# Cutting one early store into nine pieces instead of six, with other DMA engines chosen

## The chip, the core and the metric

One core of one Trainium2 chip runs the program. The metric is the device time of one execution in microseconds (us), as the median of several runs.

## What is computed

The kernel computes single-query attention and its gradients for 32 heads, 8192 keys and head size 128, all bfloat16:

```python
def _fwd_reference(q, k, v):                 # q 1x32x1x128, k and v 1x32x8192x128
    scale = q.shape[-1] ** -0.5
    scores = jnp.einsum('bhqd,bhkd->bhqk', q, k) * scale
    attn = _softmax(scores, axis=-1)
    return jnp.einsum('bhqk,bhkd->bhqd', attn, v)

def reference(q, k, v, grad_out):            # out, dq, dk, dv
    _out, _vjp = jax.vjp(_fwd_reference, q, k, v)
    return (_out, *_vjp(grad_out))
```

K and V are read once (67 MB each) and dK and dV are written once (67 MB each). With one query per head, dV is the outer product of the attention row and grad_out, and dK is the outer product of the score gradient and q.

## The kernel before, in words

The heads are handled in 16 pairs. One pair's K or V is a tile of 128 partitions, and each partition holds 128 "slots" (rows of K or V) of 128 bfloat16, so 32 KB per partition and 4096 KB per tile. The kernel has three K buffers and two V buffers. For pair j it transposes K on VectorE, computes the scores on TensorE, takes the softmax, contracts with V, and then overwrites the V tile in place with dV (`outer(j, "dv", r)`, eight steps of 16 slots each). One pair later the K tile is overwritten with dK in the same way. So a buffer is free for the next load only when its store has landed.

Nearly all DMAs are issued by SyncE (SP) in a fixed order that is written out by hand. SP works through its list in order: a DMA that has to wait for a semaphore holds back everything behind it. The part of the list around the change is: load of K of pair 2 (two halves), store of slots 64 to 127 of dV of pair 0 (L299), store of dK of pair 0 (L305), load of V of pair 2 (`load_v(2)`, L93), store of dV of pair 1 (two halves), load of K of pair 3. V of pair 2 goes into the buffer of V of pair 0, so `load_v(2)` waits until every DMA of dV of pair 0 has landed.

Slots 0 to 63 of dV of pair 0 are the exception (L296 and L297): GpSimd (POOL) issues them. They are 128 rows, one for each partition, of 16 KB each. `share_out` cuts the rows into the pieces listed in `SHARES`. An entry is (engine, first, n): the n partitions first, first + 3, first + 6 and so on go out as one DMA. The program assumes that a DMA of n rows is laid on k neighbouring DMA engines, where k is the largest divisor of n that is at most 16, beginning at a cursor that moves on by k with each GpSimd DMA. `turn_to(engine)` puts the cursor where the next piece is to begin: it issues a load of a few bytes per row into `turned` (L111) with as many rows as the cursor has to move. So each piece (L120) has one such turn ahead of it where the cursor is not yet in its place, and 128 rows can be shared unevenly among the 16 DMA engines. A SP transfer, by contrast, has 128 partitions and is shared evenly.

GpSimd DMAs take turns on eight completion semaphores. The compiled program therefore has the ninth GpSimd DMA wait until the first has landed, the tenth until the second has landed, and so on.

Of the kernel before, what the change touches and what calls it, by code (L numbers as in the profile page):

```python
# [23 lines left out]
QD = 32  # L24
LOADS = {("k", 0): 4, ("v", 0): 2, ("v", 1): 4, ("k", 2): 2}
SHARED = 64
SHARES = ((6, 12, 39), (5, 2, 42), (5, 1, 8), (15, 55, 25), (10, 25, 10), (7, 0, 4))
GP = 4


# [1 line left out]
def kernel(  # L32
# [70 lines left out]

    turned = consts.tile([17, len(SHARES), 2, 2], BF16)
    cursor = [0, 0]

    def turn_to(engine):
        n = (engine - cursor[0]) % 16
        if n:
            rows = n if n > 1 else 17  # L110
            nc.gpsimd.dma_start(turned[0:rows, cursor[1]],  # L111
                                k[0, 0].rearrange("(p n) d -> p n d", p=P)[0:rows, 0:2, 0:2])
            cursor[1] += 1
        cursor[0] = engine

    def share_out(dst, src):
        for engine, first, n in SHARES:
            turn_to(engine)
            last = first + 3 * n - 2
            nc.gpsimd.dma_start(dst[first:last:3], src[first:last:3], max_dma_last_dim=8192)  # L120
            cursor[0] = (cursor[0] + max(i for i in range(1, 17) if n % i == 0)) % 16
# [403 lines left out]
```

## Time and profile before

| | before |
|---|---|
| time, median of 3 runs | 633.09 us (632.57 to 633.21) |
| time of the profiled execution | 632.87 us |
| its span (first to last recorded work) | 631.1 us |
| VectorE busy | 516.4 us, 82% |
| TensorE matmul busy | 462.9 us, 73% |
| ScalarE busy | 205.1 us, 32% |
| GpSimd busy | 11.3 us, 2% |
| bytes moved by DMA | 268.98 MB, mean 426 GB/s over the span |
| DMA packets of SP's queue (q1) | 11232 packets, 98.5% of the time of 16 DMA engines |
| DMA packets of GpSimd's queue (q0) | 800 packets, 0.8% |

The span is 1.77 us shorter than the profiled execution's own time; what lies between is start and end of the execution, outside the recorded work. Times in the profile count from the start of the span. "Landing" is the time from the issue of a DMA until its semaphore has its full count.

### The profile page before, as it was taken

The page shows a single profiled execution, that of the slowest core. Times are in us where ns is not written, and L with a number is a line of the kernel's source. Part 1 is how long each engine was busy: PE and PEld are TensorE (multiplying, and loading weights), DVE is VectorE, ACT ScalarE, POOL GpSimd, SP SyncE. Part 2 cuts the span into 40 slices and gives each one's busy share as a digit, 9 for nine tenths or more (in the row PEclk, how much of TensorE's full clock was granted, in tenths as well). Part 3 has the DMA queues.
Part 4 walks back from the last instruction along what each step waited for, and adds up shares of the span by engine and source line. Part 5 has one row for each costly group of instructions (what it writes and reads, how often), then busy time and mean ns, then how long its engine had stood idle before and what let it go on. Part 6 is the DMA issues. An engine that isn't in the chain of part 4 may idle for free.

```text
span 631.1 us, 8018 instructions
## 1 busy us (share of the span) xinstructions
PE 462.9 (73%) x3256; PEld 245.9 (39%) x3256; DVE 516.4 (82%) x654; ACT 205.1 (32%) x460; POOL 11.3 (2%) x23
## 2 busy tenths in 40 slices
PE   4887678878787788676888757867679776697671
PEld 1443344244443425233363432624336243262441
DVE  6579997989889798796879959879697895987973
ACT  2432424043342505134052330613316142160431
POOL 2040000000000000000000000000000000000000
PEclk9789987789798977788868789777897778987785
DMA  8999999999999999999999999999999999999997
GB/s 366 433 402 436 430 428 431 429 427 440 433 427 436 436 431 433 433 432 429 429 432 429 427 433 427 433 432 418 431 430 437 436 431 425 436 427 431 428 426 336
DMA packets 12164, 268.98 MB, mean 426 GB/s; under 512 B 1856, under 2 KB 1888, under 8 KB 1888
## 3 DMA queue, kind: packets, MB, share of 16 engines
q1 hardware_dynamic: 11232, 266.34, 98.5%
q0 software_dynamic: 800, 2.12, 0.8%
q8 instruction: 25, 0.41, 0.2%
q14 instruction: 11, 0.09, 0.0%
q10 hardware_dynamic: 96, 0.02, 0.0%
HBM read 134.23 MB, written 134.23 MB: 425 GB/s over the span
## 4 chain that ended last, share of the span: by engine, by line
issue 91%; DMA 3%; PE 3%; DVE 1%; ACT 0%; POOL 0%; POOLq 0%; ACTq 0%
DMA out_dram<-Vt 2%; PE s_ps L198 1%; DMA Kt<-in_k_dram 1%; PE T_ps L215 1%; PE acc_p L265 0%; DVE XK_sb L188 0%; DVE Vt L290 0%; POOL out_dram L120 0%; DVE q_blk L174 0%; ACT p_rep L452 0%; DVE sT L205 0%; ACT win L255 0%; ACT e L440 0%; POOL turned L111 0%; POOLq L520 0%
## 5 line engine op out<-in xcount | busy, mean ns | idle before, releaser
L198 PE MATMUL s_ps<-XK_sb,q_win 128*128 128x512 bf16 x512 | 152.4, 432 | 66.6 <-DVE XK_sb L188 61.3
L290 DVE TENSOR_TENSOR Vt<-p_rep,qd 128x2048 bf16<-128x2048 bf16 x128 | 154.0, 1223 | 40.1 <-PE acc_p L265 32.2
L188 DVE STREAM_TRANSPOSE XK_sb<-Kt 128x1024 f32<-128x1024 f32 x128 | 150.2, 1218 | 37.7 <-DMA Kt<-in_k_dram 35.0
L215 PE MATMUL T_ps<-ident_f,Vt 128*128 128x128 f32 x1024 | 165.4, 314 | 6.1 <-DMA Vt<-in_v_dram 6.1
L220 ACT COPY XV_sb<-T_ps 128x512 f32<-128x512 f32 x256 | 139.6, 591 | 82.6 <-PE T_ps L215 82.4
L290 DVE TENSOR_TENSOR Kt<-ds_rep,qd 128x2048 bf16<-128x2048 bf16 x128 | 149.5, 1215 | 3.2 <-PE acc_ds L265 2.8
L215 PEld LDWEIGHTS T_ps<-ident_f,Vt 128*128 128x128 f32 x1024 | 131.2, 160 | 43.8 <-issue 18.7
L198 PEld LDWEIGHTS <-q_win 128*128 128x128 bf16 x512 | 51.6, 110 | 155.6 <-issue 123.9
L265 PE MATMUL acc_p<-Vt,win 128*32 128x512 bf16 x512 | 55.9, 439 | 2.8 <-ACT win L255 2.8
L440 ACT ACTIVATE e<-sT,nbias 128x128 f32<-128x128 f32 x16 | 8.2, 515 | 150.6 <-DVE nbias L436 150.6
L265 PEld LDWEIGHTS <-win 128*32 128x32 bf16 x1024 | 23.0, 99 | 60.6 <-issue 49.4
L265 PE MATMUL acc_ds<-Kt,win 128*32 128x512 bf16 x512 | 42.7, 429 | 4.6 <-ACT win L255 4.6
L232 PE MATMUL dp_ps<-XV_sb,do_win 128*32 128x512 bf16 x512 | 34.3, 383 | 13.5 <-ACT XV_sb L220 13.5
L255 ACT COPY win<-ds 64x128 bf16<-64x128 bf16 x32 | 9.5, 296 | 106.4 <-DVE ds L327 106.2
L232 PEld LDWEIGHTS <-do_win 128*32 128x32 bf16 x512 | 14.3, 94 | 29.2 <-issue 22.5
L441 PE MATMUL m_ps<-rs,ones_f 128*128 128x1 f32 x32 | 7.5, 305 | 24.4 <-ACT e L440 24.4
L427 PE MATMUL m_ps<-ident_f,top 128*128 128x128 f32 x16 | 4.8, 300 | 23.5 <-DVE top L425 23.5
L205 DVE STREAM_TRANSPOSE sT<-s_ps 128x512 f32<-128x512 f32 x16 | 11.5, 717 | 10.7 <-PE s_ps L198 10.7
L441 PEld LDWEIGHTS m_ps<-rs,ones_f 128*128 128x128 f32 x32 | 6.2, 242 | 27.6 <-ACT e L440 27.6
L452 ACT ACTIVATE p_rep<-e,rinv 128x512 bf16<-128x512 f32 x16 | 11.5, 722 | 13.3 <-DVE rinv L450 13.3
L427 PEld LDWEIGHTS m_ps<-ident_f,top 128*128 128x128 f32 x16 | 2.1, 133 | 31.0 <-issue 25.4
L317 PEld LDWEIGHTS m_ps<-pd,ones_f 128*128 128x128 f32 x32 | 8.2, 276 | 10.6 <-DVE prod L248 9.8
(60 smaller groups left out, 158.1 us busy)
## 6 DMA issues: line engine op xcount, KB each, us to landing
Kt<-in_k_dram SPq DMA_DIRECT2D x14, 4096.0 KB, 29.1
Vt<-in_v_dram SPq DMA_DIRECT2D x14, 4096.0 KB, 29.0
out_dram<-Kt SPq DMA_DIRECT2D x13, 4096.0 KB, 25.1
out_dram<-Vt SPq DMA_DIRECT2D x13, 4096.0 KB, 32.3
out_dram<-Vt SPq DMA_DIRECT2D x5, 2048.0 KB, 16.2
out_dram<-Kt SPq DMA_DIRECT2D x5, 2048.0 KB, 15.7
Kt<-in_k_dram SPq DMA_DIRECT2D x4, 1024.0 KB, 8.2
Vt<-in_v_dram SPq DMA_DIRECT2D x2, 2048.0 KB, 17.5
```

Of the source, the lines that this page charges most:

```text
L188: nc.vector.transpose(XK[j, u][:].rearrange("p g w i -> p (g w i)"), slots(Kt[j], u, NU).rearrange("p g d -> p (g d)").bitcast(F32))
L198: nc.tensor.matmul(st[j]["s"][:], lhsT=q_win[:, c, at:at + P], rhs=cols[:, c // 2, c % 2], start=(u == 0 and c == 0), stop=(u == NU - 1 an ...
L205: nc.vector.transpose(sT[:].rearrange("p g r -> p (g r)"), x["s"][:])
L215: nc.tensor.transpose(T_ps[:, i, :], words[:, m * P:(m + 1) * P], ident_f[:])
L220: nc.scalar.copy(XV[j][:, b * TB:(b + 1) * TB, :], st[j].pop(("T", c))[:])
L232: nc.tensor.matmul(out[b * QD:(b + 1) * QD, :], lhsT=do_win[:, b // 2, e2, at:at + QD], rhs=cols[:, z, e2, :, b * QD:(b + 1) * QD], start= ...
L255: nc.scalar.copy(win[t * M:(t + 1) * M, :, at:at + 4], src[t * M:(t + 1) * M])
L265: nc.tensor.matmul(acc[which][b * QD:(b + 1) * QD, :], lhsT=win[:, g, at:at + QD], rhs=X[:, 4 * g:4 * g + 4, :].rearrange("p n d -> p (n d)"),
L290: nc.vector.tensor_tensor(slots(G, r, NU).rearrange("p n (a b) -> p n a b", b=R), slots(rep, r, NU).unsqueeze(2).to_broadcast([P, CH, D // ...
L317: nc.tensor.matmul(x["m"][:, 1:3], lhsT=ones_f[:], rhs=x["pd"][:], start=True, stop=True, skip_group_check=True)
L441: nc.tensor.matmul(x["m"][:, 0:1], lhsT=ones_f[:], rhs=rs[:], start=True, stop=True, skip_group_check=True)
L452: nc.scalar.activation(x["p"][:], e[:].unsqueeze(2).to_broadcast([P, NT, R]), ACT.Copy, scale=rinv[:])
```

## The change

One line changes, the table of the pieces. Nothing else in the program differs: the instructions of TensorE, VectorE, ScalarE and SP are the same in the same order, and on GpSimd the twelve DMAs of `share_out` (six turns, six pieces) become eighteen (nine turns, nine pieces).

```diff
-SHARES = ((6, 12, 39), (5, 2, 42), (5, 1, 8), (15, 55, 25), (10, 25, 10), (7, 0, 4))
+SHARES = ((6, 13, 39), (6, 12, 39), (15, 29, 25), (5, 2, 7), (5, 0, 4), (7, 104, 8), (7, 1, 2), (2, 23, 2), (7, 7, 2))
```

The turns before the pieces have 6, 2, 2, 2, 6 and 3 rows before the change, and 6, 3, 12, 17, 9, 14, 8, 9 and 3 rows after it (17 rows, a prime, stand for a cursor that has to move by one). By the rule that the program assumes, the 128 rows are shared among the DMA engines like this:

| DMA engine | 0 | 1 | 2 | 3 | 4 | 5 | 6 | 7 | 8 | 9 | 10 | 11 | 12 | 13 | 14 | 15 |
|---|---|---|---|---|---|---|---|---|---|---|---|---|---|---|---|---|
| rows before | 12 | 12 | 12 | 6 | 0 | 4 | 7 | 8 | 8 | 8 | 9 | 8 | 8 | 7 | 7 | 12 |
| rows after | 11 | 11 | 12 | 6 | 0 | 2 | 8 | 11 | 11 | 8 | 8 | 8 | 7 | 7 | 7 | 11 |

## The prediction, made before the changed kernel was run

> **What bounds the kernel now.** I read the page first, its slices and queues.
>
> ```profile
> DMA  8999999999999999999999999999999999999997
> ...
> q1 hardware_dynamic: 11232, 266.34, 98.5%
> q0 software_dynamic: 800, 2.12, 0.8%
> ```
>
> The first line is the mean busy share of the 16 DMA engines in 40 slices; the two others are queue, packets, MB and share of 16 engines' time. The DMA engines are full from the second slice to the last but one, 98.5% with SP's transfers alone. So the end is set by DMA: a compute engine matters only where it leaves a DMA engine without work. Next I read GpSimd's instructions in order of time around the change (start, length, what, idle time before it), and then the landing times of the DMAs issued between 30 and 65 us (the last number).
>
> ```profile
> 32.13 0.65 POOL L120 DMA_DIRECT2D out_dram<-Vt  x1 [27.97 <-DVE Vt L290]
> 32.78 0.58 POOL L111 DMA_DIRECT2D turned<-in_k_dram  x1
> 33.35 0.62 POOL L120 DMA_DIRECT2D out_dram<-Vt  x1
> ...
> 41.53 0.56 POOL L120 DMA_DIRECT2D out_dram<-Vt  x1 [4.61 <-DMA out_dram<-Vt]
> 42.16 0.73 POOL L111 DMA_DIRECT2D turned<-in_k_dram  x1
> 45.80 0.59 POOL L120 DMA_DIRECT2D out_dram<-Vt  x1 [2.91 <-DMA out_dram<-Vt]
> ```
>
> ```profile
> out_dram<-Kt SPq DMA_DIRECT2D x1, 4096.0 KB, 21.9
> out_dram<-Vt SPq DMA_DIRECT2D x1, 2048.0 KB, 26.2
> out_dram<-Vt POOLq DMA_DIRECT2D x1, 672.0 KB, 12.2
> out_dram<-Vt POOLq DMA_DIRECT2D x1, 624.0 KB, 9.1
> out_dram<-Vt POOLq DMA_DIRECT2D x1, 400.0 KB, 21.3
> out_dram<-Vt POOLq DMA_DIRECT2D x1, 160.0 KB, 18.7
> ...
> out_dram<-Vt POOLq DMA_DIRECT2D x1, 64.0 KB, 17.3
> ```
>
> The last two pieces wait: the fifth (160 KB, 10 rows) until the first piece has landed (32.13 + 9.1 = 41.25), the sixth (64 KB, 4 rows) until the second has (33.35 + 12.2 = 45.5). The 64 KB piece then needs 17.3 us, to 63.1, though it is the smallest. Last, SP's own order of time and what SP waited for between 50 and 70 us.
>
> ```profile
> 38.77 0.35 SPq L299 DMA_DIRECT2D out_dram<-Vt  x1
> 52.89 0.34 SPq L305 DMA_DIRECT2D out_dram<-Kt  x1
> 65.04 0.34 SPq L93 DMA_DIRECT2D Vt<-in_v_dram  x1
> 73.17 4.87 SPq L305 DMA_DIRECT2D out_dram<-Vt  x2
> ```
>
> ```profile
> SPq L93 <- DMA out_dram<-Vt: 11.7, 3, 6.1
> ```
>
> SP stands at L93, the load of V of pair 2, until 65.04: first for pieces, last for its own half of dV of pair 0 (issued 38.77, landed 38.77 + 26.2 = 65.0). GpSimd's last piece had landed 1.9 us earlier.
>
> The trace also keeps start, length, size and queue of each DMA packet, but not its engine. A packet starts within a few ns of the end of the one before it on its engine, so I strung the packets into 16 streams, with the condition that each carries SP's 702 packets in SP's order. The rows of `share_out` in them come out, but for one exchanged pair of streams, as the table of the change says: one stream with 0, four with 12, one with 9. So the program's rule of cursors holds and I can name engines. Four readings carry the rest:
> - No stream has a gap of over 0.5 us between 4 and 626 us. They end between 626.4 and 629.86 us: engines 12 (629.86), 10 (629.85), 9 (629.54), 2 or a neighbour (629.1), 4 (628.9), ..., 7 and 8 (626.4). The span ends 1.24 us after the last.
> - Engine 4, without rows, is the slow one. Its 32 KB packets of stores mostly take 1.22 to 1.30 us, those of others 1.213. From the first packet of the V load of pair 2 to its end it needs 561.6 us, the others 552 to 558. It can do so because it begins that load first, at 67.28; the median stream begins at 71.8, the last (12 rows) at 74.36.
> - Every GpSimd DMA puts equally many packets on all 16 engines: where an engine has no rows, 4-byte ones stand in. By this rule there are 2 x (3+3+1+5+1+1) + 6 = 34 for the pieces, 12 for the turns, 4 for the two results, 50 in all; 16 x 50 are the page's 800.
> - While both queues have work, an engine takes one packet of GpSimd's and one of SP's by turns. A 4-byte packet thus costs GpSimd's queue an SP packet: 0.61 us at 16 KB, 1.21 us at 32 KB.
>
> **The change, part by part.**
>
> *Rows moved.* A row is two packets of 8 KB at 0.306 us, so 0.61 us. Engines 10 and 12, the two that end last, lose a row (629.86 to 629.25); engine 9 keeps its 8 and is then last at 629.54; 7 and 8 rise by 3 x 0.61 to 628.2. Gain: 0.3 us.
>
> *Three pieces and three turns more.* Issuing them costs GpSimd 6 x 0.6 us (its L120 and L111 rows), hidden, as nothing else stands in its queue until the results at 617.7. They add 15 GpSimd packets per engine, mostly of 4 bytes at 6 to 9 ns: 0.1 us.
>
> *The waits.* This is what I think decides. With eight semaphores, DMA n waits for DMA n - 8. Twelve DMAs gave waits one step deep. With eighteen, the seventh piece waits for the third (25 rows), the eighth for the fourth, and the ninth for the fifth, which had itself waited for the first. Worked out: the fifth piece is issued at 41.5 and the sixth at 45.8, as now. The third lands at 54 to 57: the 25 rows land at 56.95 now, and they have one short piece and one turn fewer ahead of them afterwards. The fifth piece, issued when the fifth is now, lands at 59 to 60.5 (now 60.24). So the ninth is issued at about 60 and its first packet can move at 63.7 (3.7 us, as the first result: issued 617.74, first packet 621.45). Ahead of its landing each engine has the queue from the seventh piece on: 3 + 2 + 3 + 2 + 3 = 13 packets, by turns with SP's. SP's packets are now those of the dK store of pair 0, 32 KB each: 13 x 1.21 = 15.7 us from the seventh piece's first packets at about 58. That is 74, and by then SP's queue has run out: its last transfer, the dK store (52.89 + 21.9), lands at 74.8, since nothing can be issued behind L93. The slowest engine finishes that store at about 74.4, after which the rest of GpSimd's packets go at once. So I take 74.4 for the landing and 74.7 for the issue of the V load, instead of 65.04. Bounds: 17.3 us as the last piece now, 60 + 17.3 + 0.1 = 77.4; and 9.1 us as the quickest piece, 60 + 9.1 + 0.9 (for the third's latest landing) = 70.
>
> A first packet follows an issue by 1.0 us where the queue is empty (first load: 0.74 to 1.75). So all 16 engines begin V of pair 2 together at 75.7. The lead of the engines with few rows is gone: engine 4 comes 75.7 - 67.28 = 8.4 us later, the median stream 3.9, those with 12 rows 1.4. Behind SP's wait stand the dV store of pair 1 (73.17 and 77.7) and the K load of pair 3 (78.1); they join a queue that V's 9.7 us keep full. VectorE and TensorE get V 1.5 to 2 us later than now (84.1), and later stores have 4 us or more of queue ahead of them, so I charge nothing more; without that cover each late store would add its own delay.
>
> *Sum.* Engine 4 ends at 628.9 + 8.4 = 637.3; the next ones are engine 9 with 629.54 + 3.9 = 633.5 and engine 10 with 633.2. Span 637.3 + 1.24 = 638.5, 7.4 us more. The profiled execution's 632.87 becomes 640.3; it lies 0.2 under the median of the runs, so 640.5 against 633.09 (+1.2%). By the bounds: 70 gives 3.7 - 0.96 = 2.8 us more than now (635.9); 77.4 gives 10.1 (643.2). The 0.96 is what engine 4 now ends ahead of the last.
>
> The Trainium skill speaks of the same landing in "DMA: Bandwidth & Descriptors", section "Anatomy of one DMA — SWDGE (gpsimd) path": about 2.0 us plus bytes over 436 GB/s. By that, an estimate from the page, the ninth piece would land at some 62 us and cost nothing. The rows above (17.3 us for 64 KB) contradict it in this loaded stretch.
>
> **The rivals.**
>
> *Late pieces land quickly.* If GpSimd's packets do not have to take turns with 32 KB packets, the ninth piece lands before 66 and only the moved rows count: last is engine 9, 632.87 - 0.3 + 0.2 = 632.8, no change. Against it: strict turns at 16 KB packets in the streams. For it: no turn with a 32 KB packet is in this trace. It decides up to an issue of the V load at 68.5; above that the loss passes 0.2% (1.2 from 65.04 until engine 4 is dry, 0.96 until it is last, 1.27 for 0.2%).
>
> *Engine 4 loses its handicap.* If its slow packets come from running ahead of the others, it keeps pace after a common start, and engine 9 is last: 633.5 + 1.24 + 1.77 + 0.2 = 636.7. For it: no slow packets before 17 us, while all run level. Against: they go on to 620 us, when its lead is gone.
>
> *Engine 7 is a slow one.* It gets the most new rows; if in unprofiled runs it ends last, 3 x 0.61 = 1.84 us come on top: 634.9. The stream with 8 rows that I take for it ends among the first. The Trainium skill, same page, section "Latency and other measured facts", calls engines 7 and 15 usually slower; this trace shows engine 4 instead.
>
> *Faster.* Engine 9 ends at 629.54 with rows unchanged, so even without any wait the gain stays near 0.3 us.
>
> **How the numbers follow.** Forecast with delayed load 0.90, engine 4 last in most of it; quick landing 0.05; engine 7 0.02; faster 0.03. The range goes from the lower bound, which takes in the handicap rival, to the upper: 635.9 to 643.2. Faster or slower counts here from 0.2%, about what a measurement of this kernel can tell from no change: slower 0.92, same 0.05, faster 0.03.
>
> **What would show it.** Right: 1040 packets in q0; three rounds of waits on GpSimd, the last piece issued near 60; the V load of pair 2 issued at 73 to 77; a dip of DMA share and GB/s between 67 and 76; a span near 638.5, with one stream ending some 4 us after the others. Wrong: the V load issued before 68.5, or no dip, or a dip of which the end shows nothing.

## The result, and the profile after

| | before | after |
|---|---|---|
| time, median of 4 runs each | 633.14 us (632.57 to 633.21) | 642.14 us (641.83 to 643.32) |
| time of the profiled execution | 632.87 us | 643.32 us |
| its span | 631.1 us | 641.5 us |

The ratio is 1.0148, with a 95% interval of 1.0132 to 1.0163: slower by 9.0 us. The prediction was 640.5 us, with 635.9 to 643.2 as its range.

The page of the kernel after: the DMA engines' mean busy share in 40 slices (16 us each here), and GpSimd's queue (packets, MB, share of the engines' time).

```profile
DMA  9999799999999999999999999999999999999996
...
q0 software_dynamic: 1040, 2.12, 0.9%
```

The fifth slice, 64 to 80 us, is now 7 tenths where it was 9. GpSimd's queue has the 1040 packets that the rule of equal rings gives for nine pieces and nine turns (16 x 65).

GpSimd in order of time after the change; in brackets what ended the wait ahead of the instruction.

```profile
45.72 0.57 POOL L120 DMA_DIRECT2D out_dram<-Vt  x1 [2.85 <-DMA out_dram<-Vt]
...
53.92 0.56 POOL L120 DMA_DIRECT2D out_dram<-Vt  x1 [7.01 <-DMA out_dram<-Vt]
...
56.97 0.56 POOL L120 DMA_DIRECT2D out_dram<-Vt  x1 [1.44 <-DMA out_dram<-Vt]
...
59.65 0.56 POOL L120 DMA_DIRECT2D out_dram<-Vt  x1 [0.87 <-DMA out_dram<-Vt]
```

The fifth piece (at 41.45) and the sixth go out when they did before. Then come the rounds that six pieces did not have: the seventh at 53.9, the eighth at 57.0, the ninth at 59.65. The landing times of the DMAs issued between 30 and 66 us (last number, us) show two of the reasons:

```profile
out_dram<-Vt POOLq DMA_DIRECT2D x1, 400.0 KB, 19.1
...
out_dram<-Vt POOLq DMA_DIRECT2D x3, 32.0 KB, 15.1
```

The 25 rows, issued at 34.57 as the third piece, land 19.1 us later, at 53.7, and release the seventh. The three pieces of 32 KB, two rows each, need 15.1 us in the median, although a row is 0.61 us of a DMA engine's time. SP's order of time, and what SP waited for between 50 and 90 us (total, times, longest):

```profile
52.87 0.34 SPq L305 DMA_DIRECT2D out_dram<-Kt  x1
74.81 0.34 SPq L93 DMA_DIRECT2D Vt<-in_v_dram  x1
```

```profile
SPq L93 <- DMA out_dram<-Vt: 21.4, 2, 19.3
```

The V load of pair 2 is issued at 74.81 instead of 65.04; SP stood 21.4 us at it, instead of 11.7. Last, the DMA engines in stretches of time, after the change and then before it. The columns are the stretch and its length, busy time of PE, PE's weight loads, DVE, ACT and POOL, PE's clock, the DMA share and GB/s.

```profile
67.00:70.00 3.00, 2.02 (x28) 0.97 (x28) 2.20 (x3) 2.62 (x8) 0.00 (x0) 1.00 0.87 374
70.00:75.00 5.00, 4.61 (x48) 2.67 (x45) 5.00 (x5) 3.01 (x7) 0.00 (x0) 1.00 0.41 169
75.00:80.00 5.00, 2.41 (x12) 0.98 (x10) 4.34 (x11) 0.00 (x0) 0.00 (x0) 1.00 0.88 315
80.00:90.00 10.00, 5.14 (x40) 2.88 (x41) 9.00 (x10) 1.14 (x3) 0.00 (x0) 0.70 1.00 387
```

```profile
70.00:75.00 5.00, 4.61 (x48) 2.65 (x45) 5.00 (x5) 3.04 (x7) 0.00 (x0) 1.00 1.00 424
80.00:90.00 10.00, 7.92 (x76) 4.95 (x80) 9.00 (x10) 4.61 (x10) 0.00 (x0) 0.83 0.98 419
```

From 67 us on the engines go dry one after the other; between 70 and 75 they are 41% busy instead of 100%. DVE is as busy as before between 70 and 75 (5.00) and between 80 and 90 (9.00). TensorE (PE) does less between 80 and 90 (5.14 instead of 7.92), because it waits 4.0 us for the late V; the streams below show that the DMA engines, and not this wait, set the end. And this is the end of the kernel after:

```profile
635.70:637.00 1.30, 0.00 (x0) 0.00 (x0) 0.00 (x0) 0.00 (x0) 0.00 (x0) 0.50 0.24 101
637.00:638.20 1.20, 0.00 (x0) 0.00 (x0) 0.00 (x0) 0.00 (x0) 0.00 (x0) 0.50 0.13 55
638.20:640.20 2.00, 0.00 (x0) 0.00 (x0) 0.00 (x0) 0.00 (x0) 0.00 (x0) 0.50 0.06 25
```

A share of 0.06 is one engine of 16. From 638.2 to 640.2 us a single engine still works.

I strung the packets of this trace into 16 streams as for the prediction. All streams begin the V load of pair 2 between 75.78 and 76.49 us. Across a stretch in which all of them are dry a stream cannot be followed from packet to packet, but the slow one can be recognised: before the stretch only the stream without rows (engine 4) has slow 32 KB packets in the dK store (1.24 to 1.28 us, nearly all others 1.213), and after it only one stream goes on with slow store packets. Taken as one, it was dry for 8.1 us and ends at 640.18, the next two end at 638.2 and 637.9, the others are done at 635.7 to 636.8. From the restart to its end the slow stream has no gap of over 0.14 us, while ten others stand without work between 610 and 631 us, for up to 1.9 us at a time. So it is this engine that sets the end. SP's last store was issued at 629.95 instead of 620.34; that the loads which feed the last pair wait for engine 4 too would explain it, but I did not follow that chain.

### The profile page after: what moved, and what is told of

It reads as the page before. It is cut to its first block, busy times and chain, and to the rows that moved or that the text cites. A ratio compares the mean times of both kernels' runs of the same rounds, so it can differ in the third digit from the quotient of the medians.

```text
span 641.5 us, 8024 instructions
## 1 busy us (share of the span) xinstructions
PE 469.7 (73%) x3256; PEld 250.5 (39%) x3256; DVE 516.7 (81%) x654; ACT 205.3 (32%) x460; POOL 15.1 (2%) x29
## 3 DMA queue, kind: packets, MB, share of 16 engines
q0 software_dynamic: 1040, 2.12, 0.9%
## 4 chain that ended last, share of the span: by engine, by line
DMA 58%; PE 28%; DVE 9%; ACT 2%; issue 1%; DVEq 0%; ACTq 0%; SPq 0%
DMA Vt<-in_v_dram 34%; PE T_ps L215 13%; DMA out_dram<-Vt 12%; PE s_ps L198 7%; DMA out_dram<-Kt 6%; DMA Kt<-in_k_dram 5%; PE acc_p L265 3%; DVE Kt L290 3%; DVE Vt L290 2%; DVE XK_sb L188 2%; ACT XV_sb L220 2%; PE dp_ps L232 1%; PE acc_ds L265 1%; PE m_ps L282 1%; DVE sT L205 1%
## 5 line engine op out<-in xcount | busy, mean ns | idle before, releaser
L198 PE MATMUL s_ps<-XK_sb,q_win 128*128 128x512 bf16 x512 | 156.1, 444 | 65.8 <-DVE XK_sb L188 61.2
L215 PE MATMUL T_ps<-ident_f,Vt 128*128 128x128 f32 x1024 | 170.0, 320 | 8.7 <-DMA Vt<-in_v_dram 8.5
L215 PEld LDWEIGHTS T_ps<-ident_f,Vt 128*128 128x128 f32 x1024 | 136.0, 164 | 46.6 <-issue 23.8
```

The source lines that it names most:

```text
L198: nc.tensor.matmul(st[j]["s"][:], lhsT=q_win[:, c, at:at + P], rhs=cols[:, c // 2, c % 2], start=(u == 0 and c == 0), stop=(u == NU - 1 an ...
L215: nc.tensor.transpose(T_ps[:, i, :], words[:, m * P:(m + 1) * P], ident_f[:])
```

## The experiments

The theory is that the third round of waits on GpSimd makes the V load of pair 2 late, that this lets all DMA engines run dry, and that the common start takes from engine 4 a lead that it needs. The rivals are that the moved rows or the extra DMAs cost by themselves, and that engine 4 is slow only while it runs ahead. All times are medians; each kernel is compared with runs of the kernel before on the same chip (632.69 us for the first four, 632.78 us for the others). The edits are shown shortened.

**More GpSimd DMAs, no row moved** (three runs, with EXTRA = 2, 4 and 6). The line numbers of these kernels are a few higher.

```diff
         for engine, first, n in SHARES:            # the table of before
+            if (engine, first, n) == SHARES[-1]:
+                for _ in range(EXTRA):
+                    nc.gpsimd.dma_start(turned[0:16, cursor[1]], ...)   # 16 rows: the cursor stays
             turn_to(engine)
```

> The six pieces of before, each row on the engine it had; two loads of 16 rows (4 bytes each, one per DMA engine, so the cursor stays) stand before the last piece's turn: 14 GpSimd DMAs. Theory (the V load of pair 2 waits for the last piece, and a late one costs engine 4 its lead): last piece lands near 65.2 instead of 63.1, V load issued at about 65.3 instead of 65.0; 633.1 to 633.5 us. Rival (moved rows or the DMAs themselves make the loss, not the lateness): 633.1, and the same in the next two.

Measured: 632.86 us, ratio 1.0001 (0.9992 to 1.0011), so this kernel does not separate the two. The last piece was down by 62.7, where I had expected 65.2, and the V load was issued at 64.99.

> As the run with fourteen GpSimd DMAs, with four such loads: 16 DMAs. Theory: third round of waits begins, last piece lands near 70, V load issued at 70, engine 4 begins it at 71.0 instead of 67.3 and ends at 632.6; 635.9 us, up to 637.4 if the stretched first and last packets that the changed kernel shows after the dry stretch come here too. Rival: 633.1.

Measured: 633.43 us, ratio 1.0035 (1.0007 to 1.0063), and the ten runs fall into two groups: seven between 632.1 and 633.7, three between 638.4 and 638.8. The profile is of a run of the first group. Its SP order of time:

```profile
65.16 0.34 SPq L94 DMA_DIRECT2D Vt<-in_v_dram  x1
```

The last piece went out at 52.9 there and was down by 63.1, so the load was not late; I had expected 70. The second group has the times of the next kernel, so I take it that the last piece was late in those runs. No profile shows it.

> As before with six such loads: 18 GpSimd DMAs as in the changed kernel, and not one row moved. Theory: V load issued at 74.5 to 75, all engines run dry, engine 4 ends last some 4 us after the next ones; 641.5 to 642.5 us, the whole loss of the change. Rival that the moved rows make the loss: 633.1. Rival that half comes from the rows: 637 to 638.

Measured: 638.71 us, ratio 1.0089 (1.0066 to 1.0113). GpSimd's last three DMAs, and the last stretch before the end:

```profile
55.51 0.51 POOL L121 DMA_DIRECT2D turned<-in_k_dram  x1 [5.97 <-DMA out_dram<-Vt]
56.75 0.58 POOL L112 DMA_DIRECT2D turned<-in_k_dram  x1 [0.74 <-DMA turned<-in_k_dram]
59.23 0.60 POOL L126 DMA_DIRECT2D out_dram<-Vt  x1 [1.90 <-DMA out_dram<-Vt]
```

```profile
632.20:636.30 4.10, 0.00 (x0) 0.00 (x0) 0.00 (x0) 0.00 (x0) 0.00 (x0) 0.50 0.06 24
```

With every row on its old engine, eighteen DMAs bring back the third round of waits, the late load and the single engine at the end: the stream with the slow store packets, which before the restart is the one without rows, ends at 636.36, the next at 631.99. Not all engines ran dry here: six streams go from the dK store to the V load without a gap. The rival of the moved rows is refuted as the main cause. The size was missed: SP issued the V load at 71.2, not at 74.5, and the loss is 6.0 us (four runs, 636.9 to 639.9), not 9. Two turns and one piece are 2 + 2 + 3 = 7 packets behind the last wait, where the change has 13; 59.2 + 3.7 + 7 x 1.21 = 71.4. This agrees with the rule of the prediction, but it was worked out when the result was known.

**A late load without GpSimd.** Only SP's list differs from before.

```diff
             for r in range(NU):                       # pair 1
                 outer(p_, "dk", r)
-            load_v(2)
 ...
             outer(j, "dv", r)
+            if (j, r) == (1, 3):
+                load_v(2)                             # behind the first half of dV's store
```

> Pieces, rows and GpSimd as before. Only SP's list differs: the V load of pair 2 stands behind the first half of the dV store of pair 1 (issued near 73) instead of ahead of it. Theory: SP's queue is dry from 67.3 (engine 4) until 74.2; engine 4 comes 6.9 us late, so 5.9 us more than before, up to 7.4 with the stretch of the restart: 638.6 to 640.5 us. Rival (lateness costs only where GpSimd's small packets are in the rings): 633.

Measured: 640.06 us, ratio 1.0118 (1.0104 to 1.0132). SP's order of time, and the last stretch:

```profile
52.57 0.34 SPq L305 DMA_DIRECT2D out_dram<-Kt  x1
72.85 0.33 SPq L305 DMA_DIRECT2D out_dram<-Vt  x1
73.41 0.34 SPq L93 DMA_DIRECT2D Vt<-in_v_dram  x1
```

```profile
636.00:637.30 1.30, 0.00 (x0) 0.00 (x0) 0.00 (x0) 0.00 (x0) 0.00 (x0) 0.50 0.06 25
```

Nothing was issued between 52.57 and 72.85, and the loss is there with GpSimd as it was: 7.3 us, in the range, and again one engine is last (0.06): the stream with the slow store packets ends at 637.37, the next at 634.99. So what costs is SP's queue running empty, whatever makes it do so.

**All engines alike.** The 128 rows go out as one DMA, eight on each engine.

```diff
-SHARES = ((6, 12, 39), ...)
+SHARES = ((0, 0, 128),)
-            nc.gpsimd.dma_start(dst[first:last:3], src[first:last:3], max_dma_last_dim=8192)
+            nc.gpsimd.dma_start(dst[0:P], src[0:P], max_dma_last_dim=8192)
```

> The 128 rows go out as one GpSimd DMA, 8 rows on every DMA engine; no turns, no waits on GpSimd. V load not late (63 to 65 us). Theory that engine 4 is slow by itself and needs its lead: its 8 rows set it back 8 x 0.61 = 4.9 us, it ends at 633.5 to 633.8, 4 us after the others; 636.7 to 637.0 us. Rival that engine 4 is slow only because it runs ahead: engine 9, 10 or 12 last at about 629.5; 632.5 to 633 us.

Measured: 637.64 us, ratio 1.0076 (1.0061 to 1.0091), 0.6 us above the range that the theory gave. SP's V load and the last two stretches:

```profile
63.94 0.34 SPq L93 DMA_DIRECT2D Vt<-in_v_dram  x1
```

```profile
629.40:631.00 1.60, 0.00 (x0) 0.00 (x0) 0.00 (x0) 0.00 (x0) 0.00 (x0) 0.50 0.24 102
631.00:634.40 3.40, 0.00 (x0) 0.00 (x0) 0.00 (x0) 0.00 (x0) 0.00 (x0) 0.50 0.06 24
```

The load is early, no engine is dry at 67 us, and still a single engine works alone for over 3 us. In the streams it is the one with the slow store packets: it ends at 634.36, the next at 630.84. All streams begin the V load within 1.6 us of each other here, so engine 4 is not slow because it runs ahead. That rival is refuted, and the 12-0-4 table of before is shown to be worth some 5 us; the 3.5 us that engine 4 ends after the next one are the larger part of it.

**The moved rows alone.** The change's table without its last three pieces; SP stores their six rows.

```diff
-SHARES = (..., (7, 104, 8), (7, 1, 2), (2, 23, 2), (7, 7, 2))
+SHARES = (..., (7, 104, 8))
+        nc.sync.dma_start(dst[1:11:3], src[1:11:3])       # after the loop of share_out
+        nc.sync.dma_start(dst[23:27:3], src[23:27:3])
```

> The changed table with its last three pieces (6 rows) taken out of GpSimd's list and issued by SP instead, as two small stores ahead of its half of dV of pair 0 (they go to the lowest-numbered DMA engines). So nearly the rows of the change (7 and 8 have 9 instead of 11, 0 and 1 have 13), but only twelve GpSimd DMAs. Theory: V load of pair 2 back at 64.5 to 65.5, engine 9 last at about 629.5; 0.3 us under before, within 632.4 to 633.1. Rival (the moved rows cost by themselves): 636 or more.

Measured: 633.46 us, ratio 1.0013 (1.0004 to 1.0022). The V load was issued at 65.94, so 8 of the 9 us are gone with the three pieces. The 0.3 us that the moved rows should gain were not seen; the kernel is 0.7 us slower than before. It isn't quite the same sharing (0 and 1 have 13 rows, and SP has two more DMAs), and I can't say which of these costs the microsecond.

**Another table of six pieces.**

```diff
+SHARES = ((5, 2, 42), (5, 0, 42), (6, 1, 14), (15, 43, 25), (14, 118, 4), (0, 126, 1))
```

> Another table of six pieces, (5,2,42), (5,0,42), (6,1,14), (15,43,25), (14,118,4), (0,126,1): by the ends of the streams of before, rows are taken from engines 9 to 12 (8, 9, 8, 8 become 7 each) and given to 0, 1, 15, 5 and 14 (13, 13, 13, 6 and 8). No third round of waits. Theory: V load at 65 to 66, ends between 625.6 and 629.0 with engines 4 and 12 last; 0.5 to 0.8 us under before. If the last piece lands after 66.3, engine 4 loses a part: no change.

Measured: 632.56 us, ratio 0.9997 (0.9988 to 1.0006): no difference. The gain of 0.5 to 0.8 us that I had expected did not come. Its streams end between 626.4 and 629.52; last is one with 13 rows that also carries packets of an instruction queue, which I had counted as one of the early ones. Taking rows from the last engines made another engine the last, 0.3 us earlier in this profile than in that of before (629.86), which the times do not show.

**Smaller packets after the dry stretch.** The changed kernel, with the late load in four DMAs.

```diff
-LOADS = {("k", 0): 4, ("v", 0): 2, ("v", 1): 4, ("k", 2): 2}
+LOADS = {("k", 0): 4, ("v", 0): 2, ("v", 1): 4, ("k", 2): 2, ("v", 2): 4}
```

> The changed kernel with the V load of pair 2 cut into four DMAs, so its packets have 8 KB instead of 32 KB. In the changed kernel this load takes each DMA engine 11.1 to 11.9 us instead of 9.7, with a long first and a long eighth packet. Theory A: the stretch belongs to restarting all engines from dry, whatever the packets: again 1.4 us or more, 641.5 to 642.5 us. Theory B: it belongs to 32 KB packets starting in step: 0.5 us or less remain, 640.5 to 641.2 us.

Measured: 642.45 us, ratio 1.0156 (1.0143 to 1.0170), theory A. The stretches that answer to those above:

```profile
75.00:80.00 5.00, 3.76 (x30) 1.69 (x25) 4.00 (x11) 0.70 (x3) 0.00 (x0) 1.00 0.89 339
80.00:90.00 10.00, 6.90 (x80) 4.68 (x81) 9.25 (x10) 4.32 (x10) 0.00 (x0) 0.99 1.01 374
```

The restart is as slow with 8 KB packets (339 and 374 GB/s, after 315 and 387). In the streams the first part takes 2.5 to 3.2 us, the second and third 2.5 each, and the last 3.1 to 4.1, so there is a second slow spell at the end of the load, whatever the packets' size. It does not go by the time since the restart: with the late load by SP the last two packets of the V load are the long ones too (up to 1.7 and 1.9 us), and there they start 13 to 15 us after the restart at 73.7.

## Why the prediction was right

- *Waits.* Right in each step: the fifth and sixth piece unmoved (41.45, 45.72), the third landing at 53.7 (54 to 57 given), the ninth issued at 59.65 (about 60), the V load at 74.81 (74.7). The landing follows from packets taken by turns: the three pieces of 32 KB took 15.1 us. On at least 15 of the 16 streams GpSimd's last packets come right behind the last packet of the dK store, which on the last engine ended at 74.22. So the turns held GpSimd's packets back until SP's queue had run out, as the prediction had it. By an estimate from the Trainium skill's figure ("DMA: Bandwidth & Descriptors", section "Anatomy of one DMA — SWDGE (gpsimd) path") the last piece would have been down near 62; under this load it was not.
- *Dry engines.* First packets at 75.78 (75.7), the median stream dry for some 4 us, engine 4 for 8.1 (8.4). The late load by SP alone shows that this is what costs.
- *Engine 4 last.* Right: alone for the last 2 us after the change. The even table shows that its handicap is its own. The prediction's argument for the other view, no slow packets before 17 us, had no force: the slow packets are those of stores, and the first store is issued at 32 us.
- *Sum.* 9.0 us instead of 7.4. The term that was too small is the one for the load itself, "V's 9.7 us": after the dry stretch this load took each engine 11.1 to 11.9 us, 11.4 on engine 4, so 1.7 us more there. I had charged nothing for the restart. With it the last engine has V at 87.8 instead of 84.1, 3.7 us later, where the prediction had 1.5 to 2. The profiled execution is 1.2 us above the median of its runs, and has engine 4 another 1.1 us later than the sum and the restart give; what makes that is open.
- *Moved rows.* Their 0.3 us stayed unproved: one kernel with nearly these rows in time was 0.13% slower, another table equal.
- *Rivals.* Quick landing failed: the strict turns seen with 16 KB packets hold with 32 KB packets too. Engine 7 is not the one that ends last: that is the slow stream, which has no rows before the dry stretch. This goes against the other rule taken from that page of the Trainium skill (section "Latency and other measured facts"). Which of the other streams is engine 7 after the stretch, the packets do not tell.

## What to carry to other kernels

In a kernel bound by DMA, look first at whether an edit can leave the issuing queue empty: count what is queued behind each wait, and compare the latest issue with the time at which the fastest engine has used up its queue. Cutting a transfer into more pieces is not a matter of bytes: each DMA from GpSimd takes turns with the large packets on every engine and, past eight, waits for an earlier one. When engines are loaded unevenly on purpose, a common stop undoes it, and the price is the lead of the slowest engine, not the mean idle time; here a slow restart came on top.

## What the runs showed of the hardware that was not expected

- After all engines had been dry, the first 32 KB packet took 1.5 to 2.2 us instead of 1.21 and the eighth, some ten us later, 1.8 to 2.3; the load took 11.1 to 11.9 us instead of 9.7. The 2048 KB store that ends the dry stretch in the kernel with the late load by SP landed after 7.4 us, against 4.9 us of packets. The second spell, at the end of the V load, stands in all four traces in which that load came late; what makes it is open.
- One of the 16 DMA engines is slower with stores from beginning to end: in the trace of before, 1.241 us in the median for its 32 KB store packets (most have 1.22 to 1.30) where the others have 1.213, but 1.214 for its loads. In the even kernel it ends 3.5 us after the next one. It is the stream without rows in the kernel with fourteen GpSimd DMAs and in the other table of six pieces too, which ran on two chips.
- With sixteen GpSimd DMAs the same program took 632.1 to 633.7 us in seven runs and 638.4 to 638.8 in three. That the last piece came in time in the seven and late in the three is inferred; the only profile is of one of the seven.
